# Moving one fill step between two value products, one load and one transpose in an attention and mixer kernel

## The chip, the cores and the metric

The kernel runs on one core of a Trainium2 chip. The metric is device time in microseconds of one execution. The kernel before the change took 580.42 us (median of 4 runs, 580.39 to 581.01). One of these four executions, the one of 581.01 us, was taken by the hardware profiler; its span in the trace is 579.2 us, so 1.8 us lie around it.

## The reference

Eight batches, twelve heads, 448 rows, head size 64. First a cosine attention, then a mixer over its output:

```python
q_n = q / (norm(q) + 1e-6); k_n = k / (norm(k) + 1e-6)
attn = softmax(q_n @ k_n.T / tau)          # per batch and head
x = (attn @ v), heads side by side          # 8 x 448 x 768
h = x.transpose(0, 2, 1) @ U @ V            # rank 32 over the rows
u = x + h.transpose(0, 2, 1)
out = u + relu(u @ w_ch1) @ w_ch2           # 768 -> 3072 -> 768
```

## The kernel before

**Work and units.** Two heads make a pair, six pairs a batch (NP = 6), 48 pairs in all. Loads come in groups of two pairs (gi 4 and later; group 6 holds pairs 10 and 11, group 7 pairs 12 and 13). A group's q, k and v are loaded by SyncE (SP) into one of three buffer sets, squared on GpSimd (L243), summed on VectorE (L248), turned into roots on ScalarE (L253, L254), inverted on VectorE (L260, L262), scaled on GpSimd (L268); v is cast on GpSimd (L276). For each pair the scaled q and k are transposed, from pair 12 on by a DMA that SP issues (step_T, L315). Scores are matmuls (L331, L343) and ScalarE takes their exponent (L353, L356). The product with the values comes in two halves, V(n, 0) and V(n, 1) (L412 and L419, or L393). Each half is divided by its sums on VectorE: L430 and L431 in the first form, L398 and L399 in the second. The result X is transposed by a DMA of SP (L500). step_A2 (L508) multiplies U with X of two pairs; step_H2 (L523, L528) multiplies that with V and adds the transposed X, which gives u.

**Fill steps.** The mixer of the batch before is cut into fill steps of six matmuls: 24 of the first product (L570), each followed by a relu to SBUF on ScalarE (L575) or VectorE (L577), and the second product in steps of six (L598), four steps to a chunk, each chunk closed by an addition on VectorE (o_sb, L617) and two output DMAs of SP (L623, L627 or L630). Each fill group writes one of two PSUM banks, in turn (new_m, L540). step_A2 takes the bank that the last group did not take (own_bank, L545), and so its first matmul needs the eviction of the group before the last.

**Order.** The order on every engine is written out by hand. From n = 6 on, the main loop goes through slots, one for each pair n. An even slot with n of at least 14 runs the list at L905 to L912: the scores of the last quarter and of quarters 0 and 1, V(n-1, 0), then V(n-1, 1) with its transpose, then A2(n-2) with further scores, then V(n, 0), then V(n, 1). spread (L841) runs this list and puts the slot's nf fill steps between its items: after item i, it has given nf times the sum of the weights so far, divided by the sum of all weights (17) and rounded down. put (L793) hangs further steps at a place (n, i): after item i of slot n; the index -1 is ahead of the slot. In an odd late slot, (n, 0) comes after the scores 1 and 2 and step_H2. Instructions of one engine run in program order; an instruction waits on semaphores for what it reads and for the buffers it overwrites. Every DMA of SP also waits until the DMA eight places ahead of it in SP's order has landed, since SP's DMAs use eight semaphores in turn.

**Weights.** GpSimd issues the loads of w1 in four parts (L168) and of w2 in four parts (L173), each 1152 KB: the third part of w1 ahead of slot 6, the fourth at (6, 2), the first half of w2 at (6, 3), the second half at (7, 2). load_copies (L159, L162) is at (8, 2): three loads of V into V_raw by SP.

Of the kernel before, what the change touches and what calls it, by code (L numbers as in the profile page):

```python
# [22 lines left out]
def kernel(  # L23
# [23 lines left out]
    NP = H // 2  # L47
# [233 lines left out]
    def by_dma(n):  # L281

        return n >= 2 * NP
# [25 lines left out]
    def step_T(b, p):  # L309
        if not by_dma(b * NP + p):  # L310
            pe_T(b, p)
            evict_T(b, p)
            return
        gi, j = group_of[(b, p)]
        nc.sync.dma_start_transpose(  # L315
            out=new_qkT(b, p).rearrange("p a (c r) -> p (a c) r", r=128),
            in_=norm[gi][0][:, j, :, :, :, :].rearrange("p i c h d -> p (i c h d)"))
# [119 lines left out]
    def step_V(b, p, half):  # L437
        if (b, p, half) in av_of:
            close_V(b, p, half)
            return  # L440
        if half == 1 and b * NP + p >= FIRST2:
            bank = psum.tile([128, 512], FP, name="up", tag="ps_x", bufs=1)
        else:
            bank = psum.tile([128, 512], FP, name="av", tag="ps_av", bufs=1)
        pe_V(b, p, half, bank)
        divide_V(b, p, half)
# [205 lines left out]
    def f(n):  # L652
        for _ in range(n):
            fill.pop(0)()
# [13 lines left out]
    def T(n):  # L668
        step_T(*pairs[n])

    def Sc(n, *cs):
        step_S(*pairs[n], cs)

    def V(n, half):
        step_V(*pairs[n], half)

    def A(n):
        step_A(*pairs[n])

    def Hs(n):  # L680
        step_H(*pairs[n])
# [111 lines left out]
    def put(n, at, fn):  # L793
        after.setdefault((n, at), []).append(fn)

    for gi in range(5, len(groups)):
        m, g = first_pair[gi], preps[gi]
        if m == NP + 2:
            at = [(NP, 1), (NP, 2), (NP + 1, 6), (NP, 3), (NP, 5), (NP, 6)]
            when = (NP + 1, 0)  # L800
        elif m == NP + 4:
            at = [(NP + 2, 0), (NP + 2, 1), (NP + 4, 0), (NP + 2, 4), (NP + 2, 6), (NP + 2, 7)]
            when = (NP + 3, 0)
        elif m == 2 * NP:
            at = [(m - 3, 6), (m - 3, 6), (m - 1, 0), (m - 3, 6)] + [(m - 2, i) for i in (0, 1)]
            when = (m - 2, 2)
        elif m == 2 * NP + 2:
            at = [(m - 2, i) for i in (0, 0, 5, 3, 4, 5)]
            when = (m - 2, 5)
        else:  # L810
            at = [(m - 3, 0), (m - 3, 0), (m - 3, 5)] + [(m - 2, i) for i in (0, 1, 2)]
            when = (m - 2, 3)

        put(*at[0], lambda g=g: g.square(0))
        put(*at[1], lambda g=g: g.square(1))
        put(*at[2], lambda g=g: g.values())
        put(*at[3], lambda g=g: g.reduce(0))
        put(*at[4], lambda g=g: g.reduce(1))
        put(*at[5], lambda g=g: g.root())
        put(*when, lambda g=g: (g.invert(), [g.scale(i, j, P_) for j in (0, 1) for i in (1, 0)]))  # L820
        if gi > 5 and m - 6 <= NP:
            at = (((NP, 3), (NP, 3), (NP + 2, 0)), ((NP + 3, 0), (NP + 3, 0), (NP + 4, 4)))[gi - 6]
            for x, w in zip("qkv", at):
                put(*w, lambda gi=gi, x=x: load(gi, x, nc.sync))
        elif gi > 5:
            at = {2 * NP + 2: [(m - 3, i) for i in (0, 1, 3)],
                  2 * NP + 4: [(m - 4, i) for i in (0, 2, 4)]}.get(m, [(m - 6, 4), (m - 5, 5), (m - 4, 3)])
            for x, w in zip("qkv", at):
                put(*w, lambda gi=gi, x=x: load(gi, x, nc.sync))
        if by_dma(m):  # L830
            first = m == 2 * NP
            put(*((m - 2, 6) if first else (m - 1, -1)), lambda m=m: T(m))
            put(m - 1, -1, lambda m=m: T(m + 1))

    put(NP, 2, lambda: load_w1(2304, 3072))
    put(NP, 3, lambda: (load_w2(0, 0, 12), load_w2(0, 12, 24)))
# [4 lines left out]
    def spread(n, order, nf, first=0):  # L841

        weights = [w if fn is not False else 0 for w, fn in order]
        given = acc = 0
        for i, ((_, fn), w) in enumerate(zip(order, weights)):
            if fn:
                fn()
            for g in after.pop((n, i + first), []):
                g()
            acc += w  # L850
            want = nf * acc // sum(weights)
            f(min(want - given, len(fill)))
            given = want

    KEEP = 3
    for n in range(NP, NPAIR + 1):
        b, p = pairs[n] if n < NPAIR else (B, 0)
        now, nxt = n < NPAIR, n + 1 < NPAIR
        done = n > NP
        late = n > FIRST2  # L860
        for g in after.pop((n, -1), []):
            g()
        state_of["busy"] = n == NP + 1
        if not late:
            if n % 2 == 0:

                order = [
                    (1, lambda: Sc(n, 0, 1)),
                    (0, done and (lambda: V(n - 1, 0))),
                    (1, None if by_dma(n + 1) else (lambda: T(n + 1))),  # L870
                    (0, lambda: Sc(n, 3)),
                    (1, (lambda: V(n - 1, 1)) if done else None),
                    (0, done and (lambda: A(n - 1))),
                    (1, lambda: (Sc(n, 2), Sc(n + 1, 0))),
                    (1, (lambda: Hs(n - 1)) if done else None),
                ]
            else:
                order = [
                    (1, lambda: Sc(n, 1, 2)),
                    (1, lambda: V(n - 1, 0)),  # L880
                    (0, lambda: Sc(n, 3)),
                    (1, lambda: V(n - 1, 1)),
                    (1, not by_dma(n + 1) and (lambda: T(n + 1))),
                    (1, lambda: A(n - 1)),
                    (0, lambda: Hs(n - 1)),
                ]
            last = p == 0 and done
            nf = len(fill) if last else 5
            spread(n, order, nf)
            if last:  # L890
                f(len(fill))
                fill.extend(steps_m1(b - 1) + steps_m2(b - 1))
            continue

        def X2(m):
            step_XT(*pairs[m])

        def A2(m):
            step_A2(*pairs[m], now and m + 2 >= FIRST4)

        def H2(m):
            step_H2(*pairs[m])

        if n % 2 == 0 and now and n >= FIRST4:
            order = [  # L905
                (3, lambda: (step_S3(*pairs[n]), Sc(n, 0, 1))),
                (1, lambda: V(n - 1, 0)),
                (4, lambda: (V(n - 1, 1), X2(n - 1))),
                (4, lambda: (A2(n - 2), Sc(n, 2), Sc(n + 1, 0), open_V(*pairs[n]))),
                (2, lambda: V(n, 0)),  # L910
                (3, lambda: (V(n, 1), X2(n))),
            ]  # L912
            spread(n, order, int(round((len(fill) - KEEP) / (1 + (-p) % NP))))
            continue
        if n % 2 == 0:
            order = [
                (2, now and (lambda: (n >= FIRST4 and step_S3(*pairs[n]), Sc(n, 0, 1)))),
                (2, lambda: V(n - 1, 0)),
                (2, lambda: (V(n - 1, 1), X2(n - 1))),
                (2, None if n >= FIRST4 else (lambda: Sc(n, 3))),  # L920
                (3, lambda: (A2(n - 2), now and (Sc(n, 2), Sc(n + 1, 0)))),
                (2, not now and (lambda: H2(n - 2))),
            ]
            nf = len(fill) if not now else int(round((len(fill) - KEEP) / (1 + (-p) % NP)))
            spread(n, order, nf)
            if not now:
                f(len(fill))
                fill.extend(steps_m1(b - 1) + steps_m2(b - 1))
            continue
        Sc(n, 1, 2)  # L930
        if n - 3 >= FIRST2:
            H2(n - 3)
        for g in after.pop((n, 0), []):
            g()
        if p == 1 and n - 2 > FIRST2:
            f(len(fill))
            fill.extend(steps_m1(b - 1) + steps_m2(b - 1))
        order = [
            (2, None if n > FIRST4 else (lambda: V(n - 1, 0))),
            (2, None if n > FIRST4 else (lambda: Sc(n, 3))),  # L940
            (2, None if n > FIRST4 else (lambda: (V(n - 1, 1), X2(n - 1)))),
            (2, None),
            (2, None),
        ]
        nf = int(round((len(fill) - KEEP) / (1 + (-p) % NP)))
        f(2)
        spread(n, order, nf - 2, 1)
# [37 lines left out]
```

## Time and profile before

| What | Before |
|---|---|
| Median of 4 runs | 580.42 us |
| The profiled execution | 581.01 us |
| Its span | 579.2 us |
| TensorE busy | 567.0 us |
| TensorE weight loads busy | 330.3 us |
| ScalarE, VectorE, GpSimd busy | 262.0, 213.3, 213.9 us |
| L570 matmuls, one | 353 ns, 1128 of them |
| L598 matmuls, one | 323 ns, 1368 of them |
| Granted TensorE clock | 0.999 |
| Loads of w1 and w2, issue to landing | median 18.5 us |
| Loads of v by SP, 128 KB, issue to landing | median 2.8 us |

A matmul's duration is the time from its start to the modelled end of its pipeline, so consecutive matmuls overlap: in a run of L570 they start 0.19 us apart. An idle time beside an instruction counts from the modelled end of the one before it, so it is shorter than what the start was late by. Times are those of the one profiled execution.

### The profile page before, as it was taken

Reading aid. Unit: us, or ns where it says so; the run is one execution under the profiler, and the core shown is the slowest. Engines: PE = TensorE matmul, PEld = TensorE weight load, DVE = VectorE, ACT = ScalarE, POOL = GpSimd, SP = SyncE. Lnnn points to the kernel's source line nnn. Section 1 sums busy time; section 2 is a strip of 40 time slices with the busy share of each in tenths; the row PEclk is TensorE's granted clock in tenths of the full one; section 3 lists DMA queues with packets and bytes.
Section 4 is the critical chain, followed back from the end, with each engine's and each line's share of the span. In section 5 each row is a group of like instructions: output and inputs, shape, how many; then the busy total and the mean of one; then the engine's idle time right before and its main releaser. Section 6 shows DMA issues by size and latency. Waiting matters only on the chain.

```text
span 579.2 us, 12651 instructions
## 1 busy us (share of the span) xinstructions
PE 567.0 (98%) x5302; PEld 330.3 (57%) x5302; DVE 213.3 (37%) x460; ACT 262.0 (45%) x449; POOL 213.9 (37%) x202
## 2 busy tenths in 40 slices
PE   6999999999999999999999999999999999999997
PEld 5665566555655556555556555555566555655565
DVE  6874551433343324524235233433243331320011
ACT  5877544465333653445424465336433365214200
POOL 8747564724416236416145064253261420000000
PEclk9999999999999999999999999999999999999999
DMA  6899999686367465574464663674545612222022
GB/s 164 190 234 236 238 210 210 180 163 153 93 141 148 104 146 122 131 158 108 94 150 134 132 146 99 134 171 99 119 112 132 132 38 55 51 55 50 7 50 55
DMA packets 139882, 74.53 MB, mean 129 GB/s; under 512 B 86688, under 2 KB 139696, under 8 KB 139824
## 3 DMA queue, kind: packets, MB, share of 16 engines
q1 hardware_dynamic: 129568, 63.20, 48.4%
q0 software_dynamic: 9632, 10.01, 10.2%
q8 instruction: 41, 0.67, 0.5%
q10 hardware_dynamic: 624, 0.51, 0.3%
q14 instruction: 17, 0.14, 0.1%
HBM read 52.19 MB, written 11.01 MB: 109 GB/s over the span
## 4 chain that ended last, share of the span: by engine, by line
PE 83%; DMA 8%; DVE 3%; SPq 2%; ACT 1%; issue 1%; POOL 1%; DVEq 0%; POOLq 0%; ACTq 0%
PE mp L598 36%; PE mp L570 32%; PE sc L331 5%; DMA w_sb<-in_moe_w_ch_dram 5%; PE av L419 2%; DMA kst<-in_k_dram 1%; DMA qst<-in_q_dram 1%; DVE ss L248 1%; PE av L393 1%; PE up L419 1%; PE up L393 1%; PE av L343 1%; PE mp L508 1%; DVE X L431 1%; PE av L523 1%
## 5 line engine op out<-in xcount | busy, mean ns | idle before, releaser
L598 PE MATMUL mp<-w_sb,relu 128*128 128x384 bf16 (+2 forms) x1368 | 234.5, 323 | 0.9 <-DMA w_sb<-in_moe_w_ch_dram 0.9
L598 PEld LDWEIGHTS <-relu 128*128 128x128 bf16 x1368 | 126.5, 98 | 85.3 <-issue 10.1
L570 PEld LDWEIGHTS <-w_sb 128*128 128x128 bf16 x1128 | 106.0, 98 | 99.6 <-issue 7.2
L356 ACT ACTIVATE E<-sc 128x896 bf16<-128x896 f32 x144 | 125.1, 922 | 54.1 <-PE sc L331 52.9
L575 ACT ACTIVATE relu<-mp 128x448 bf16<-128x448 f32 x163 | 88.2, 543 | 119.5 <-PE mp L570 119.5
L268 POOL TENSOR_TENSOR qk<-kst,inv 128x512 bf16<-128x512 f32 x43 | 45.9, 1069 | 238.4 <-DVE inv L262 231.1
L570 PE MATMUL mp<-uO,w_sb 128*128 128x448 bf16 x576 | 113.6, 353 | 0.0
L570 PE MATMUL mp<-uE,w_sb 128*128 128x448 bf16 x552 | 111.4, 353 | 0.0
L617 DVE TENSOR_TENSOR o_sb<-mp,ut 128x384 f32<-128x384 f32 (+2 forms) x51 | 28.0, 549 | 140.2 <-PE mp L598 126.8
L248 DVE TENSOR_REDUCE ss<-sq 128x16 f32<-128x1024 f32 (+1 forms) x50 | 57.7, 1166 | 1.8 <-ACT sq L240 1.0
L577 DVE TENSOR_SCALAR relu<-mp 128x448 bf16<-128x448 f32 x25 | 15.6, 625 | 100.2 <-PE mp L570 99.7
L268 POOL TENSOR_TENSOR qk<-qst,inv 128x512 bf16<-128x512 f32 x44 | 47.3, 1077 | 1.9 <-PE up L480 1.9
L331 PE MATMUL sc<-qkT 64*64 64x448 bf16 x576 | 42.7, 360 | 0.6 <-ACT E L356 0.3
L243 POOL TENSOR_TENSOR sq<-kst 128x1024 f32<-128x1024 f32 (+1 forms) x23 | 42.6, 1854 | 0.2
L243 POOL TENSOR_TENSOR sq<-qst 128x1024 f32<-128x1024 f32 x21 | 39.7, 1892 | 7.3 <-DMA qst<-in_q_dram 7.3
L276 POOL CAST v<-vst 128x1024 bf16<-128x1024 f32 (+1 forms) x25 | 25.4, 1017 | 11.9 <-DMA vst<-in_v_dram 8.8
L419 PEld LDWEIGHTS <-E 128*128 128x128 bf16 x744 | 29.1, 97 | 0.0
L353 ACT ACTIVATE E<-av 128x448 bf16<-128x448 f32 x17 | 9.2, 541 | 42.4 <-PE up L343 28.6
L331 PEld LDWEIGHTS <-qkT 64*64 64x64 bf16 x576 | 12.7, 105 | 14.3 <-issue 8.6
L393 PEld LDWEIGHTS <-E 128*128 128x128 bf16 x408 | 17.3, 97 | 5.0
L419 PE MATMUL av<-v,E 128*128 128x65 bf16 x420 | 18.9, 193 | 0.0
L253 ACT ACTIVATE ss<-ss,tiny 128x32 f32<-128x32 f32 (+1 forms) x25 | 8.0, 321 | 18.0 <-DVE ss L248 18.0
(109 smaller groups left out, 367.7 us busy)
## 6 DMA issues: line engine op xcount, KB each, us to landing
out_dram<-o_sb SPq DMA_DIRECT2D x108, 96.0 KB, 2.2
w_sb<-in_moe_w_ch_dram POOLq DMA_DIRECT2D x8, 1152.0 KB, 18.5
qst<-in_q_dram SPq DMA_DIRECT2D x23, 256.0 KB, 3.8
vst<-in_v_dram SPq DMA_DIRECT2D x46, 128.0 KB, 2.8
kst<-in_k_dram SPq DMA_DIRECT2D x44, 128.0 KB, 2.8
qst<-in_q_dram SPq DMA_DIRECT2D x23, 192.0 KB, 3.9
vst<-in_v_dram SPq DMA_DIRECT2D x46, 96.0 KB, 2.6
kst<-in_k_dram SPq DMA_DIRECT2D x44, 96.0 KB, 2.7
```

What stands on the lines that cost most here:

```text
L243: nc.gpsimd.tensor_mul(sq[:, 0:self.nh * 4, :], self.flat(t), self.flat(t))
L248: nc.vector.reduce_sum(self.ss[:, j, 0:self.nh * 4], self.sq[j][:, 0:self.nh * 4, :], axis=AX.X)
L268: eng.tensor_mul(qks[self.gi % 2][:, j, i, :, :, :], t[:, 2 * j:2 * j + 2, :, :].rearrange("p h c d -> p c h d"), iv.unsqueeze(3).to_broad ...
L276: nc.gpsimd.tensor_copy(out=self.flat(v65[self.s])[:, :, 0:D], in_=self.flat(vst[self.s]))
L331: nc.tensor.matmul(out=sc[o:o + 64, h, 0:S], lhsT=t[r, 1, c * 128 + o:c * 128 + o + 64], rhs=t[r, 0, 0:S], start=True, stop=True)
L356: nc.scalar.activation(out=e[:, 2 * c:2 * c + 2, 0:S], in_=sc[:, :, 0:S], func=AF.Exp)
L393: nc.tensor.matmul(out=av[:, ic, :], lhsT=e[:, 2 * c + h, ic * 128:(ic + 1) * 128], rhs=vv[:, 2 * j + h, c, :], start=False, stop=(ic == 3 ...
L419: nc.tensor.matmul(out=av[:, i, h, :], lhsT=e[:, 2 * c + h, ic * 128:(ic + 1) * 128], rhs=vv[:, 2 * j + h, c, :], start=False, stop=(i == ...
L570: nc.tensor.matmul(out=mp, lhsT=w1_sb[:, cc, f * 128:(f + 1) * 128], rhs=u[:, cc, 0:S], start=(cc == 0), stop=(cc == CC - 1))
L575: nc.scalar.activation(out=relu[:, f, o:o + S], in_=mp, func=AF.Relu)
L598: nc.tensor.matmul(out=mp, lhsT=relu[:, f, r0:r0 + 128], rhs=w2_sb[:, f, half * HC + c0:half * HC + c1], start=(f == 0), stop=(b > 0 and f ...
L617: nc.vector.tensor_add(o.rearrange("p (k d) -> p k d", d=128), mp.rearrange("p (k d) -> p k d", d=128), ut_of[(b, half)][:, c0 // 128:c1 / ...
```

## The change

Three edits.

1. The loads of q and k of group 6 are put at (7, 0) in place of (6, 3), and the load of its v at (8, 4) in place of (8, 0).
2. The transpose of the second pair of a group, T(m + 1), is put at (m - 1, 0) in place of (m - 1, -1), for all groups transposed by DMA but the first.
3. In the even slots from 14 on, the weight behind V(n-1, 0) is 2 in place of 1, and behind V(n-1, 1) it is 3 in place of 4. The sum stays 17.

```diff
         if gi > 5 and m - 6 <= NP:
-            at = (((NP, 3), (NP, 3), (NP + 2, 0)), ((NP + 3, 0), (NP + 3, 0), (NP + 4, 4)))[gi - 6]
+            at = (((NP + 1, 0), (NP + 1, 0), (NP + 2, 4)), ((NP + 3, 0), (NP + 3, 0), (NP + 4, 4)))[gi - 6]
...
             first = m == 2 * NP
             put(*((m - 2, 6) if first else (m - 1, -1)), lambda m=m: T(m))
-            put(m - 1, -1, lambda m=m: T(m + 1))
+            put(m - 1, -1 if first else 0, lambda m=m: T(m + 1))
...
                 (3, lambda: (step_S3(*pairs[n]), Sc(n, 0, 1))),
-                (1, lambda: V(n - 1, 0)),
-                (4, lambda: (V(n - 1, 1), X2(n - 1))),
+                (2, lambda: V(n - 1, 0)),
+                (3, lambda: (V(n - 1, 1), X2(n - 1))),
                 (4, lambda: (A2(n - 2), Sc(n, 2), Sc(n + 1, 0), open_V(*pairs[n]))),
```

## The prediction

> **What bounds the kernel now.** I read the page first, then the waits of TensorE, then its timeline slot by slot. On the page:
>
> ```profile
> PE 567.0 (98%) x5302; PEld 330.3 (57%) x5302; DVE 213.3 (37%) x460; ACT 262.0 (45%) x449; POOL 213.9 (37%) x202
> ...
> PE 83%; DMA 8%; DVE 3%; SPq 2%; ACT 1%; issue 1%; POOL 1%; DVEq 0%; POOLq 0%; ACTq 0%
> ```
>
> TensorE is busy 567.0 of 579.2 us and holds 83% of the chain. No other engine is over 45%. The change adds and removes no instruction, so it can only open or close gaps on TensorE. From 60 us on, its waits of 0.5 us and more in sum are these (sum, times, longest):
>
> ```profile
> PE mp L598 <- DMA w_sb<-in_moe_w_ch_dram: 0.9, 1, 0.9
> PE mp L508 <- DVE o_sb L617: 0.8, 2, 0.4
> PE mp L508 <- ACT relu L575: 0.5, 3, 0.2
> ```
>
> One wait for w2, and five at A2 (L508), which wants the bank of the fill group before the last.
>
> **Edit 3, the weights.** In the built order the fill steps move in 8 of the 17 slots: n = 20, 22, 24, 32, 34, 36, 44, 46. They have nf = 7: behind V(n-1, 0) stand 7x4/17 = 1 step before (the one ahead of it) and 7x5/17 = 2 after; behind V(n-1, 1) both have 7x8/17 = 3. The other nine have nf = 9: 9x4/17 and 9x5/17 are both 2. So in eight slots one fill step of six matmuls passes from behind V(n-1, 1) to between the halves. All five L508 waits lie in these slots. The neighbours with nf = 9 already have a step between the halves and show the price without a wait. Slot 16, first half and A2:
>
> ```profile
> 148.56 0.28 PE L412 MATMUL av<-v,E 128*128 128x130 bf16 x2
> ...
> 152.57 0.30 PE L508 MATMUL mp<-X,U_sb 128*32 128x128 bf16 x8
> ```
>
> That is 4.01 us with three L598 steps of 0.97 us (150.03 - 149.06), so 3.04 us with two. Slot 24 has two:
>
> ```profile
> 235.19 0.28 PE L412 MATMUL av<-v,E 128*128 128x130 bf16 x2
> ...
> 236.45 1.21 DVE L248 TENSOR_REDUCE ss<-sq 128x16 f32<-128x1024 f32 x1
> ...
> 237.58 0.17 DVE L430 RECIPROCAL rd<-up 128x4 f32<-128x4 f32 x1
> ...
> 237.79 0.42 DVE L431 TENSOR_TENSOR X<-up,rd 128x256 bf16<-128x256 f32 x1
> ...
> 238.13 0.55 DVE L617 TENSOR_TENSOR o_sb<-mp,ut 128x384 f32<-128x384 f32 x1
> ...
> 238.73 0.30 PE L508 MATMUL mp<-X,U_sb 128*32 128x128 bf16 x8 [0.42 <-DVE o_sb L617]
> ```
>
> 238.73 - 235.19 = 3.54, so A2 is 0.50 us late. The first step behind the halves is the last of a chunk; its o_sb stands on VectorE behind the reduce and the divide.
>
> *Slots 20, 32, 44* (L570 steps). Slot 14 takes 4.49 us from V(n-1, 0) to A2 (124.47 to 128.96) with three steps of 1.13 (126.10 - 124.97), so 3.36 with two. Slot 20 takes 3.60:
>
> ```profile
> 194.69 0.28 PE L412 MATMUL av<-v,E 128*128 128x130 bf16 x2
> ...
> 195.18 0.28 PE L412 MATMUL up<-v,E 128*128 128x130 bf16 x2
> ...
> 197.22 0.32 ACT L253 ACTIVATE ss<-ss,tiny 128x32 f32<-128x32 f32 x1 [1.23 <-DVE ss L248]
> ...
> 197.71 0.98 ACT L575 ACTIVATE relu<-mp 128x448 bf16<-128x448 f32 x2
> ...
> 198.29 0.30 PE L508 MATMUL mp<-X,U_sb 128*32 128x128 bf16 x8 [0.18 <-ACT relu L575]
> ```
>
> A2 is 0.24 us late; by the starts to the nanosecond, L508 follows the last fill matmul by 529 ns in these three slots and by 283 ns in slot 14, so 0.246 us. Cause: the first step's relu stands on ScalarE behind the root (L253), which waits for the reduce. In the new order that relu stands ahead of the root. The moved step starts at 195.18, where the second half started, and ends by about 196.5; ScalarE is idle from 195.99 to 197.22, so the relu (0.54) ends near 197.0, and A2 comes at 198.04. The wait goes. What is late next: the second half ends 1.13 us later, at 196.97, and its divide starts at 197.10 in any case, behind the reduce: hidden with 0.13 us to spare. A2's seventh matmul needs that X, ready at 197.73: 0.3 us to spare. Gain 3 x 0.246 = **0.74 us**.
>
> *Slots 24, 36* (L598, o_sb). L508 follows 750 ns behind, against 256 in slot 16: 0.494 late. In the new order of VectorE, o_sb stands ahead of the second half's divide. It starts at 237.58 and ends at 238.13, in time. But the same work remains: the divide starts 0.49 later (an o_sb is followed 0.49 later at 420.25), its product 0.21 after that, and takes 0.42: X ready at 238.70. A2's seventh matmul now waits for this X (a new wait in the built program; queued behind it on TensorE are the eighth and the next scores) and starts at 238.75. Before, it started 0.07 after 238.73, at 238.80. Gain 0.05 each, **0.10 us**. Bounds: 0 and 0.494 each. I take the low value, since VectorE's five rows add up to the same end. SP's transpose of X (L500) now follows the two output DMAs: by their rows it issues some 1.2 us later, at 239.4, and lands near 242.0 to 243.1; H2 wants it at 244.9.
>
> *Slots 22, 34, 46.* 219.30 - 216.26 = 3.04: no wait before. The second half then ends at 218.39, the divide starts at 218.68: hidden. Gain 0.
>
> **Edit 2, the transposes.** In the built program SP's sequence and the semaphore counts of these transposes stay as they were: nothing of SP's stands between the two places, and the overwritten buffer was read in the slot before. 0 us. The waits at slots 30 and 42 (transpose landed 0.14 and 0.40 us behind the time of the scores) follow from H2, so they move along and stay.
>
> **Edit 1, the loads.** No SP instruction stands between (6, 3) and (7, 0), and SP doesn't wait for slots: q and k of group 6 keep their places, their waits and their issue at 46.30 to 49.66. What moves is v: its four DMAs (448 KB) now stand behind the three of V_raw (168 KB). The seven are released by the same landings as before: V_raw at about 51.3, 52.7 and 55.2, v at 57.8 to 62.1; the loads of q and k of group 7 behind them then start at 63.05 as before or up to a microsecond earlier. v lands before about 72 and is cast at 80.32: hidden, and the cast's queue with it. On the path is only w2:
>
> ```profile
> 51.10 28.69 DMA w_sb<-in_moe_w_ch_dram
> ...
> 79.84 1.14 PE L598 MATMUL mp<-w_sb,relu 128*128 128x384 bf16 x6 [0.89 <-DMA w_sb<-in_moe_w_ch_dram]
> ```
>
> ```profile
> 60.00:70.00 10.00, 10.00 (x105) 5.84 (x103) 5.52 (x10) 5.42 (x11) 5.84 (x5) 1.00 1.23 241
> ...
> 76.00:80.00 4.00, 3.11 (x34) 2.18 (x31) 1.30 (x3) 0.73 (x3) 4.00 (x3) 1.00 1.31 204
> ```
>
> (The last column is GB/s.) SP's loads have all landed by 76.07, 3.7 us ahead of this part of w2. The same bytes stand ahead of it in either order, and the DMA engines are busy for nine tenths and more from 29 to 101 us (the page's slices). So 0 us. Bounds: the wait's whole 0.82 us gained (start 820 ns late), or lost what the bytes cost that now come later: the difference, 280 KB at 239 GB/s (50 to 60 us), is 1.2 us; all 616 KB are 2.6 us.
>
> A row first: the same v loads take 8.9 to 12.6 us to land here and 2.8 at the median, though w2 is on GpSimd's queue and v on SP's. The Trainium skill ("DMA: Bandwidth & Descriptors", Issuing engines are not separate DMA queues) says that DMAs of different issuing engines run on the same 16 engines and interleave. That speaks against a queue left to w1: by it, a later load gives the weights a share and takes it back. By strict queues w2 would gain nothing, by sharing up to the stated bound; the sum stays.
>
> **Sum.** 0.74 + 0.10 + 0 + 0 = 0.84 us. The profiled execution goes from 581.01 to 580.17 (span 578.4); it is 0.59 above the median of the four runs, so from 580.42 I forecast **579.58 us**, 0.14% less. A measurement of this kernel tells about 0.2%, 1.16 us, from no change.
>
> **Rivals.**
> - *w2's wait goes too* (0.12): lighter loads ahead from 51 to 58 us. For: TensorE waits there alone for a DMA. Against: bytes are only swapped. 580.42 - 0.84 - 0.82 = 578.8.
> - *Slots 24 and 36 give back all* (0.10): if X is ready sooner than the rows add up to. 580.42 - 0.74 - 0.99 = 578.7.
> - *The waits come back later* (0.10): A2 earlier by 0.25, then the scores behind it wait for ScalarE, or margins of 0.06 (slot 22: X at 219.31, wanted 219.37) and 0.13 fail. 580.4.
> - *Slower, by one mechanism* (0.10): v's 448 KB, now issued at 57.8 to 62.1, take their share while the second part of w2 is moving, and it lands later; each microsecond counts in full at 79.84. From 0.84 us late on the kernel is slower; with 1.2 us 580.8, with 2.6 us 582.2. Against: 3.7 us of margin.
>
> **How the numbers follow.** Forecast 0.58, rivals 0.42 as given. 578.6 to 580.8 holds all but the upper part of the slower rival and a little measurement spread. Faster by over 0.2% (below 579.26): the first two rivals and 0.03 of the forecast, 0.25. Slower by over 0.2% (above 581.58): over half of the last rival, 0.06. Within: 0.69.
>
> **What would show it.** In the profile after: the L508 wait on relu gone, that on o_sb replaced by one on X of about the same length within A2; SP's q and k of group 6 still near 46 to 50 us; w2's wait near 0.9. I am wrong if L508 waits in slots 20, 32, 44, if w2 lands over half a microsecond away from 79.8, or if a new wait over 0.2 us stands in these eight slots.

## The result and the profile after

The changed kernel took 579.83 us (median of 34 runs, 578.83 to 581.43), the kernel before 580.56 us (55 runs, 579.84 to 582.37): ratio 0.9987, 95% interval 0.9982 to 0.9991. That is 0.75 us less (0.5 to 1.0). A ratio of 1 lies outside the interval, but the difference is smaller than the 0.2% that the prediction took as the bound of no change. The forecast was 579.58 us, 0.84 us less, with a range of 578.6 to 580.8. The profiled execution of after took 579.85 us, its span is 578.1 us.

From the page of after, busy times and the chain by engine:

```profile
PE 567.4 (98%) x5302; PEld 330.4 (57%) x5302; DVE 212.7 (37%) x460; ACT 262.2 (45%) x449; POOL 213.7 (37%) x202
...
PE 85%; DMA 8%; SPq 2%; DVE 2%; POOL 1%; issue 1%; ACT 0%; POOLq 0%; DVEq 0%
```

TensorE runs the same 5302 matmuls; its share of the chain is two points larger and that of VectorE one smaller. The waits of TensorE from 60 us on (sum, times, longest):

```profile
PE mp L598 <- DMA w_sb<-in_moe_w_ch_dram: 0.5, 1, 0.5
PE mp L508 <- DVE X L431: 0.4, 2, 0.2
```

A2's three waits for a relu (0.5 us in sum before) are gone. The two for o_sb are now two for X. The timeline of slot 20, TensorE and ScalarE:

```profile
194.44 0.28 PE L412 MATMUL av<-v,E 128*128 128x130 bf16 x2
...
194.94 1.29 PE L570 MATMUL mp<-uE,w_sb 128*128 128x448 bf16 x6
...
196.07 0.28 PE L412 MATMUL up<-v,E 128*128 128x130 bf16 x2
...
196.19 0.54 PE L419 MATMUL up<-v,E 128*128 128x65 bf16 x12
196.27 0.54 ACT L575 ACTIVATE relu<-mp 128x448 bf16<-128x448 f32 x1 [0.53 <-PE mp L570]
...
196.85 0.17 DVE L430 RECIPROCAL rd<-up 128x4 f32<-128x4 f32 x1
196.97 0.32 ACT L253 ACTIVATE ss<-ss,tiny 128x32 f32<-128x32 f32 x1 [0.16 <-DVE ss L248]
...
197.79 0.30 PE L508 MATMUL mp<-X,U_sb 128*32 128x128 bf16 x8
```

The fill step stands between the halves, its relu runs at 196.27, ahead of the root at 196.97, and A2 comes without a wait: 3.35 us after the first half in place of 3.60. The second half ends at 196.73, its divide starts at 196.85: 0.12 us to spare, where 0.13 had been worked out. Slot 24:

```profile
234.70 0.28 PE L412 MATMUL av<-v,E 128*128 128x130 bf16 x2
...
237.08 0.55 DVE L617 TENSOR_TENSOR o_sb<-mp,ut 128x384 f32<-128x384 f32 x1
...
237.55 0.17 DVE L430 RECIPROCAL rd<-up 128x4 f32<-128x4 f32 x1
...
237.74 0.29 PE L508 MATMUL mp<-X,U_sb 128*32 128x128 bf16 x6
237.75 0.42 DVE L431 TENSOR_TENSOR X<-up,rd 128x256 bf16<-128x256 f32 x1
...
238.23 0.23 PE L508 MATMUL mp<-X,U_sb 128*32 128x128 bf16 x2 [0.20 <-DVE X L431]
```

A2 now starts in time, but its seventh matmul starts 0.42 us behind the sixth, when X is there. From the last fill matmul to the scores behind A2 it was 750 + 226 = 976 ns and is 255 + 654 = 909. SP's transpose of this X was issued at 238.92, behind the two output DMAs, and step_H2's additions, the first at 244.58 (L528), waited for the matmuls ahead of them (L523) as before, and not for it.

### The profile page after: what moved, and what is told of

The parts are those of the page before. It is cut to its first block, busy times and chain, and to the rows that moved or that the text cites. A ratio compares the mean times of both kernels' runs of the same rounds, so it can differ in the third digit from the quotient of the medians.

```text
span 578.1 us, 12651 instructions
## 1 busy us (share of the span) xinstructions
PE 567.4 (98%) x5302; PEld 330.4 (57%) x5302; DVE 212.7 (37%) x460; ACT 262.2 (45%) x449; POOL 213.7 (37%) x202
## 4 chain that ended last, share of the span: by engine, by line
PE 85%; DMA 8%; SPq 2%; DVE 2%; POOL 1%; issue 1%; ACT 0%; POOLq 0%; DVEq 0%
PE mp L598 36%; PE mp L570 33%; PE sc L331 5%; DMA w_sb<-in_moe_w_ch_dram 5%; PE av L419 2%; DMA kst<-in_k_dram 2%; PE up L419 1%; PE av L393 1%; PE up L393 1%; PE av L343 1%; PE mp L508 1%; DMA vst<-in_v_dram 1%; DMA qst<-in_q_dram 1%; PE av L523 1%; PE av L412 1%
## 5 line engine op out<-in xcount | busy, mean ns | idle before, releaser
L331 PE MATMUL sc<-qkT 64*64 64x448 bf16 x576 | 42.7, 360 | 0.6 <-ACT E L356 0.3
L419 PEld LDWEIGHTS <-E 128*128 128x128 bf16 x744 | 29.1, 97 | 0.0
L353 ACT ACTIVATE E<-av 128x448 bf16<-128x448 f32 x17 | 9.2, 541 | 42.4 <-PE up L343 28.6
L331 PEld LDWEIGHTS <-qkT 64*64 64x64 bf16 x576 | 12.8, 105 | 14.2 <-issue 8.6
L393 PEld LDWEIGHTS <-E 128*128 128x128 bf16 x408 | 17.3, 97 | 5.0
L412 PEld LDWEIGHTS <-E 128*128 128x128 bf16 x124 | 11.4, 98 | 9.0 <-issue 1.0
```

The source lines that it names most:

```text
L331: nc.tensor.matmul(out=sc[o:o + 64, h, 0:S], lhsT=t[r, 1, c * 128 + o:c * 128 + o + 64], rhs=t[r, 0, 0:S], start=True, stop=True)
L393: nc.tensor.matmul(out=av[:, ic, :], lhsT=e[:, 2 * c + h, ic * 128:(ic + 1) * 128], rhs=vv[:, 2 * j + h, c, :], start=False, stop=(ic == 3 ...
L419: nc.tensor.matmul(out=av[:, i, h, :], lhsT=e[:, 2 * c + h, ic * 128:(ic + 1) * 128], rhs=vv[:, 2 * j + h, c, :], start=False, stop=(i == ...
```

## The experiments

Ratios are to the kernel before, from runs on the same chip. "The A2 rows" are the distances from the last fill matmul to A2 in slots 20, 32, 44 and in slots 24, 36: 529 and 750 ns before.

**e1_weights**: edit 3 alone.

> The kernel before with the third edit alone (weights 2 and 3 in place of 1 and 4). Theory A, that of the prediction: edit 3 carries the whole gain, 0.84 us by its sum (three waits of A2 for a relu gone, 0.74; two waits on o_sb replaced by waits on X, 0.10), so about 0.13 to 0.15% less than before; A2 follows the last fill matmul by 283 ns in slots 20, 32, 44, and inside A2 a gap of about 0.42 us stands in slots 24 and 36; the wait for w2 stays at 0.8 to 0.9 us. Rival B: part of the gain comes from the order of V_raw and v, whose w2 landed 0.30 us earlier in the profile after; then edit 3 alone gives some 0.4 to 0.5 us only, since whatever it gains is not touched by w2 but the measured 0.75 us has to be shared.

Measured: 579.92 us, ratio 0.9986 (0.9978 to 0.9994). The A2 rows are 283 and 256, with 0.42 us inside A2 in slots 24 and 36, as in after. Edit 3 alone gives what the whole change gives; the interval is too wide to leave out the 0.4 to 0.5 us of rival B by the time alone. The w2 wait did not stay: in this profile there is none, though V_raw and v stand as before.

**e2_loads**: edits 1 and 2 alone.

> The kernel before with the first and second edit alone (loads of group 6, transposes). Theory A: 0 us, within 0.05%; the five waits at A2 stay (529 ns three times, 750 ns twice), q and k of group 6 are issued near 46 to 50 us as before, V_raw ahead of v. Rival B: 0.3 to 0.4 us less, with the second part of w2 landing at about 79.5 in place of 79.8 and the wait behind it halved. Rival: slower by up to 1.2 us if v, now issued at 57.8 to 62, takes its share from w2.

Measured: 580.81 us, ratio 1.0002 (0.999 to 1.0013): no difference shown; the interval reaches from 0.6 us less to 0.75 us more. The A2 rows are 526 to 528 and 749 to 750. q and k of group 6 were issued from 45.45 us on (46.30 before), V_raw at 50.23, 51.78 and 54.51, v from 57.18. The w2 wait is absent here too, as it was in e1_weights with the old order, so it is not the order that makes or removes it, and rival B loses its ground, though the interval alone would allow its 0.3 to 0.4 us. A loss of 1.2 us lies outside the interval. From issue to landing this part of w2 took 28.3 to 29.4 us with the old order (five profiles) and 28.3 to 28.6 with the new (four).

**e3_root**: the kernel before with a later root.

```diff
-            at = [(m - 3, 0), (m - 3, 0), (m - 3, 5)] + [(m - 2, i) for i in (0, 1, 2)]
+            at = [(m - 3, 0), (m - 3, 0), (m - 3, 5)] + [(m - 2, i) for i in (0, 1, 3)]
             when = (m - 2, 3)
```

> The kernel before, with the root of the next group put one item later, behind A2 and its scores (the weights stay 1 and 4). It tells why A2 waits for a relu in slots 20, 32, 44. Theory A: the relu of the first step stands behind the root on ScalarE, and the root waits for the reduce; with the root behind A2 the relu runs at once, A2 follows the last fill matmul by 283 ns, and 3 x 0.246 = 0.74 us go, 0.13% less than before; the o_sb waits of slots 24 and 36 stay at 750 ns. Rival C: A2 is simply too close behind the step whose bank it takes, and only a larger distance helps; then the three waits stay at 529 ns and the time is that of before. The root's delay of about 3 us moves scales and transposes, which have 2 to 5 us of margin in most slots.

Measured: 582.84 us, ratio 1.0033 (1.002 to 1.0046): slower, which neither theory had. The A2 rows are 282 to 283 and 748 to 749, as theory A says of the wait. The loss is elsewhere; TensorE's waits of e3_root from 60 us on, and slot 14 in its timeline:

```profile
PE mp L598 <- DMA w_sb<-in_moe_w_ch_dram: 1.7, 1, 1.7
PE mp L570 <- DVE relu L577: 1.1, 3, 0.4
PE mp L508 <- DVE o_sb L617: 0.8, 2, 0.4
PE up L343 <- DMA qkT<-qk: 0.8, 2, 0.6
```

```profile
132.85 0.23 ACT L254 ACTIVATE ss<-ss 128x32 f32<-128x32 f32 x1
133.12 0.18 DVE L260 TENSOR_SCALAR ss<-ss 128x32 f32<-128x32 f32 x1 [4.37 <-ACT ss L254]
...
133.60 1.09 DVE L577 TENSOR_SCALAR relu<-mp 128x448 bf16<-128x448 f32 x2
...
134.22 1.29 PE L570 MATMUL mp<-uO,w_sb 128*128 128x448 bf16 x6 [0.36 <-DVE relu L577]
```

The inverse (L260) kept its place and waited 4.37 us for the late root; VectorE did nothing meanwhile, and the relus queued behind it freed their banks late. By starts that costs 0.52 us in slots 14, 26, 38 and 0.14 in slots 20, 32, 44, and the transposes were 0.93 and 0.63 us late in slots 30 and 42, where before they were 0.18 and 0.44: -0.74 + 1.55 + 0.41 + 0.94 = 2.2 us, against 1.9 measured. (The w2 wait of this execution is not in the sum.)

**e9_root_inverse**: as e3_root, and `when = (m - 2, 4)`.

> The kernel before with the root one item later, as in e3_root, and the inverse one item later as well (item 4). It tells what made e3_root slower. Theory A': in e3_root the inverse stood on VectorE right behind the late root and held VectorE for 4.4 us, so relus behind it freed their banks late (0.52 us three times, 0.14 three times) and the transposes came later; with the inverse behind the value half these waits go, and what is left is the gain that e3_root was meant to show: A2 follows by 283 ns in slots 20, 32, 44, 3 x 0.246 = 0.74 us, 0.13% less than before; the o_sb waits stay at 750 ns. Rival: the late root itself costs the time (transposes late for the next scores); then the time stays above that of before by some 0.1 to 0.3%.

Measured: 580.34 us, ratio 0.9993 (0.9984 to 1.0002). The relu waits on VectorE are gone, the A2 rows are 282 and 750 to 751: in the trace the reading of e3_root holds. The time is inconclusive: the interval holds no change and the 0.13%. The transposes of slots 30 and 42 were 0.47 and 0.67 us late in this execution; in e2_loads, where the root wasn't moved, they were 0.50 and 0.56, so one profile can't say whether the late root took part.

**e4_reduce**: the kernel after, with the second reduce moved behind A2, and root and inverse behind the next value half.

```diff
-            at = [(m - 3, 0), (m - 3, 0), (m - 3, 5)] + [(m - 2, i) for i in (0, 1, 2)]
-            when = (m - 2, 3)
+            at = [(m - 3, 0), (m - 3, 0), (m - 3, 5)] + [(m - 2, i) for i in (0, 3, 4)]
+            when = (m - 2, 4)
```

> The kernel after, with the second reduce of the next group put behind A2 (item 3 in place of 1), and root and inverse behind the next value half (item 4). It tells what holds A2's seventh matmul in slots 24 and 36. Theory A: VectorE's work ahead of X is what counts; without the reduce (1.13 us) ahead of it o_sb and X are ready in time, the gaps of 0.42 us inside A2 go and 2 x 0.42 = 0.84 us are gained on top of after: about 578.9 to 579.0 us, 0.27 to 0.30% less than before. Rival D: the gap is made by the second half coming a step later on TensorE, or the delayed inverse makes the transposes late at the next scores; then no gain over after, or a new wait at the scores of slots 18, 24, 30, 36 or 42.

Measured: 578.58 us, ratio 0.9961 (0.9949 to 0.9973); the 0.27 to 0.30% lies at the near end of the interval. Compared matmul by matmul, the scores behind A2 come 0.43 us earlier against after in each of slots 24 and 36, as expected. Slot 24 in its timeline:

```profile
236.43 0.56 DVE L617 TENSOR_TENSOR o_sb<-mp,ut 128x384 f32<-128x384 f32 x1 [0.33 <-PE mp L598]
236.93 0.18 DVE L430 RECIPROCAL rd<-up 128x4 f32<-128x4 f32 x1
237.15 0.42 DVE L431 TENSOR_TENSOR X<-up,rd 128x256 bf16<-128x256 f32 x1
237.49 1.21 DVE L248 TENSOR_REDUCE ss<-sq 128x16 f32<-128x1024 f32 x1
...
237.80 0.30 PE L508 MATMUL mp<-X,U_sb 128*32 128x128 bf16 x8
```

With the reduce behind them, o_sb is done 0.8 us and X 0.2 us ahead of A2, which runs in one piece.

**e6_reduce_before**: the same edit in the kernel before, with its weights 1 and 4.

> The kernel before (weights 1 and 4, loads and transposes as before) with the second reduce behind A2 and root and inverse behind the next value half, as in e4_reduce. It tells whether the weights of edit 3 matter by themselves. Theory A: the five waits come from reduce and root ahead of the evictions, in VectorE's and ScalarE's order; with these moved, A2 follows by 283 ns and 256 ns in all slots though no fill step stands between the halves: 1.73 us less than before, as e4_reduce (0.30 to 0.39% less). Rival C: without a step between the halves the second half's X or the eviction is late all the same; then part of the waits stays and edit 3 is needed.

Measured: 578.37 us, ratio 0.9958 (0.9943 to 0.9972). The A2 rows are 282 and 256, and no gap is left inside A2, with no fill step between the halves. Rival C falls: the place of the fill step matters only while reduce and root stand ahead of the evictions.

**e5_split**: the kernel after, with the load of the second quarter of w2 in two parts.

```diff
-    put(NP, 3, lambda: (load_w2(0, 0, 12), load_w2(0, 12, 24)))
+    put(NP, 3, lambda: (load_w2(0, 0, 12), load_w2(0, 12, 18), load_w2(0, 18, 24)))
```

> The kernel after, with the second quarter of w2 loaded in two DMAs of 576 KB (its first six blocks, then the last six) in place of one of 1152 KB. It tells what the wait for w2 is worth, on which the prediction put the bounds of edit 1. Theory A: the order of V_raw and v doesn't set this wait; it is set by how much of w2 must land before the first needed block. That block then lands at about 76.2 (72.9 and half of 6.6 us), 2.9 us ahead of its use near 79.1: the wait is gone in the profile. It was 0.82, 0.41, 0, 0, 1.63 and 0.37 us in the profiles of the six kernels so far, which issue that load at 50.2 to 51.6 us, 0.54 on average: about 0.5 us less than after, some 0.2% less than before in all. Rival: the wait is no loss in most executions, or its time comes back later; then the time is that of after.

Measured: 579.39 us, ratio 0.9978 (0.9968 to 0.9987). The first part landed at 76.27, and the wait is gone. The median is 0.44 us below that of after, near the 0.5, but the intervals of the two ratios overlap.

**e7_t_early**: e4_reduce with both transposes at (m - 2, 5).

```diff
-            put(*((m - 2, 6) if first else (m - 1, -1)), lambda m=m: T(m))
-            put(m - 1, -1 if first else 0, lambda m=m: T(m + 1))
+            put(*((m - 2, 6) if first else (m - 2, 5)), lambda m=m: T(m))
+            put(*((m - 1, -1) if first else (m - 2, 5)), lambda m=m: T(m + 1))
```

> e4_reduce, with both transposes of the next pairs put at (m - 2, 5), behind the last X of the even slot, so ahead of the last output DMAs in SP's order. It tells what makes the transposes late for the scores of slots 30 and 42 (waits of 0.37 to 0.39 us in e4_reduce, from 0.1 to 0.5 in the other profiles). Theory A: SP's order; two output DMAs (1.2 us) go ahead of the transposes and after the X transpose, so the transposes land about 1.2 us earlier and the waits go: 0.7 to 0.8 us less than e4_reduce. Rival: the transposes wait for something else (scales on GpSimd, the X transpose) and nothing changes, or the output DMAs behind them free their buffers too late and VectorE's o_sb waits: slower.

Measured: 578.10 us, ratio 0.9953 (0.9938 to 0.9968). SP's timeline ahead of slot 42 in e7_t_early:

```profile
429.71 1.45 SPq L500 DMA_TRANSPOSE XT<-X  x1
431.27 2.62 SPq L315 DMA_TRANSPOSE qkT<-qk  x2
433.95 0.59 SPq L623 DMA_DIRECT2D out_dram<-o_sb  x1
```

The transposes follow the X transpose at once, where in e4_reduce two output DMAs stood between (430.63, 432.21, 432.85, 433.55). No wait for them is left in the profile: the scores of slots 30 and 42 come 0.39 and 0.37 us earlier than in e4_reduce. The 0.48 us between the medians is not resolved by the intervals.

**e8_all**: e7_t_early with the split load of e5_split.

> e7_t_early and the split load of e5_split together. Theory A: the gains add, since they are separate waits of TensorE: about 0.5 us less than e7_t_early; against before 0.84 + 0.84 + 0.75 + 0.5 = 2.9 us, 0.5% less. Rival: one gain is taken back by the next wait; then no more than the better of the two.

Measured: 577.53 us (577.39 to 577.71), ratio 0.9943 (0.9927 to 0.9958), 0.57% less where 0.5% was expected: the lowest median of all, faster than before and after. Its interval overlaps those of e4_reduce, e6_reduce_before, e7_t_early and e10_all_old. From 60 us on, its profile has no wait of TensorE to list.

**e10_all_old**: e8_all with edits 1 and 3 taken back.

> e8_all with edits 1 and 3 taken back (weights 1 and 4, loads of group 6 as before). Theory A: with reduce, root and inverse out of the way no eviction is late at A2, so the weights are worth nothing, and the loads' order never was: the time of e8_all within 0.05% (577.5 us). Rival: a step between the halves still helps somewhere; then up to 0.8 us more than e8_all.

Measured: 577.82 us, ratio 0.9951 (0.9939 to 0.9963), overlapping that of e8_all. The A2 rows are 282 to 283 and 256, as in e8_all. From 21 us on, every score matmul (L331) starts 0.08 to 0.09 us later than in e8_all, and TensorE's last matmul ends at 572.17 in place of 572.08 us. So on TensorE the two differ by 0.01 us at most over all that edits 1 and 3 touch; of the 0.22 us between the two profiled executions, 0.09 lie ahead of that and the rest comes after the last matmul.

## Why the prediction was right, by its steps

- *Slots 20, 32, 44.* Right in cause and size: 529 to 283 ns, three times. The cause, root ahead of relu, is shown by e3_root, e9_root_inverse and e6_reduce_before, which move the root and not the fill step.
- *Slots 24, 36.* Right: 0.067 and 0.062 us in place of 0.05 each. The new wait stands at A2's seventh matmul; in e4_reduce, with the reduce behind o_sb and X, it is gone. The rival in which these slots give back all didn't come.
- *Slots 22, 34, 46.* Right: 255 to 256 ns before, 256 after. Nor did the gains come back as later waits: the scores behind each of the five A2 keep their lead, and the last scores of all start 1.15 us earlier in after than in before.
- *Edit 2.* Right as far as e2_loads shows, where it stands together with edit 1; the two were not run apart. SP's order around these transposes is the same before and after. The prediction let their waits follow from H2; e7_t_early shows that they go when two output DMAs of SP no longer stand between the X transpose and them.
- *Edit 1.* Right in that q and k don't move (45.76 to 49.12 us in after); that the order is worth nothing is as e2_loads and e10_all_old have it. One step was misjudged: "w2's wait near 0.9" took one execution's wait for a fixed row, and "820 ns late" was too low. What shows how late the matmuls start is the distance from the fill step before them, in before and in e1_weights:

```profile
77.39 1.14 PE L598 MATMUL mp<-w_sb,relu 128*128 128x384 bf16 x6
...
79.84 1.14 PE L598 MATMUL mp<-w_sb,relu 128*128 128x384 bf16 x6 [0.89 <-DMA w_sb<-in_moe_w_ch_dram]
```

```profile
77.74 1.14 PE L598 MATMUL mp<-w_sb,relu 128*128 128x384 bf16 x6
...
79.14 1.14 PE L598 MATMUL mp<-w_sb,relu 128*128 128x384 bf16 x6
```

  It is 2.45 us in before and 1.40 where nothing is waited for, so the start was 1.05 us late in before. In the same way it was 0.64 late in after, 1.87 in e3_root, 0.60 in e4_reduce, 0.14 or less in e6_reduce_before, e7_t_early and e9_root_inverse, and 0 in e1_weights and e2_loads: old and new order on both sides. (The average of the six profiles that e5_split's expectation uses is then 0.69 and not 0.54.) The size goes by when GpSimd issues that load. The chain of after shows what stands ahead of it:

```profile
38.18 8.99 DMA kst<-in_k_dram
...
47.33 1.89 POOL sq L243
49.22 0.82 POOL w_sb L168
50.04 1.00 POOL w_sb L173
51.04 28.46 DMA w_sb<-in_moe_w_ch_dram
79.50 0.04 issue
79.55 1.14 PE mp L598 x6
```

  GpSimd squares k and issues the weights after that; in all nine profiles without the split load the issue follows the start of this square by 3.7 us, and the load takes 28.3 to 29.4 us. Issued at 51.0 to 51.6 us (before, after, e3_root, e4_reduce) it is waited for by 0.6 us and more, at 50.2 to 50.7 (the other five) by 0.14 at most. What holds the square back differs from profile to profile (in after the landing of k), and no run moved it by itself. So the 1.15 us between the two profiled executions is not the change alone: 0.74 and 0.13 are, 0.41 is this wait, and TensorE's start 0.11 us later in after takes some back. The change's 0.87 by the trace and the 0.75 by the medians (0.5 to 1.0) agree.
- *The Trainium skill.* "DMA: Bandwidth & Descriptors" (Issuing engines are not separate DMA queues) says that DMAs interleave whoever issues them. The long landing times of v beside w2 (8.9 to 12.6 us) fit it; e2_loads, with 28.29 us for w2 against 28.69 before and no change of the time shown, doesn't test it, since the bytes were only swapped. "Perfetto Trace Analysis" (Optimization Strategy) says that a gap that repeats can mean too few buffers for the next tile. Here the gap repeated in five slots, and e6_reduce_before closed it with the same two banks, by the order on the evicting engines. So the page's "can" is not a "must": here the order was enough, and more banks were not tried.

What stays open: whether edits 1 and 2 have effects too small for e2_loads, what makes GpSimd's issue of w2 early or late, and what part of the half microseconds of e5_split and e7_t_early holds beyond their intervals.

## What to carry to other kernels

A repeated short wait for a bank is read from the queue of the engine that empties it: look for what stands ahead of the eviction there and takes time or waits for something else. Moving that (ratio 0.9958, 0.9943 to 0.9972) was worth more here than giving the eviction more time (0.9987, 0.9982 to 0.9991). When an instruction that produces is put off, put off its consumer on the in-order engine as well, or the consumer holds up all behind it, as in e3_root for 4.37 us. A load moved in program order doesn't move in time unless something on its own queue stands between the two places, as q and k of group 6 here.

## What the runs showed that was not expected

GpSimd issued the second quarter of w2 at 50.2 to 51.6 us, 1.4 us apart from one profiled execution to the next, though no kernel changes anything ahead of that. Where TensorE waits for the load at 79 us, the difference stays to the end: before was 0.35 us ahead of e1_weights at 72 us and 0.69 behind it at 87. Without that wait (with the split load) the executions of e8_all lie within 0.32 us (6 runs) and those of e10_all_old within 0.9 (5 runs), but those of e5_split within 1.7 (12 runs), against 2.5 for the kernel before (55 runs): this wait is not all that makes executions differ.
